# A fused attention and feed-forward kernel: the lag between the two row halves carried through the down tiles and across batches, scales moved to the outputs, plain evictions

## The chip, the cores and the metric

The kernel runs on one core of one Trainium2 chip. The metric is the device time of one execution in microseconds. The kernel before was timed three times: 424.82, 425.56 and 425.59 us, median 425.56. Engines are called as in the profile: PE (TensorE matmuls; PEld its weight loads), DVE (VectorE), ACT (ScalarE), POOL (GpSimd) and SP (SyncE, which issues output and transpose DMAs).

## The reference

Grouped attention (8 batches, 16 query heads on 4 key heads, 384 positions, head size 64) is followed by a feed-forward layer on the 3072 x 1024 result:

```python
scores = (1.0 / np.sqrt(D)) * np.matmul(q, k.transpose(0, 1, 3, 2))
attn = np.exp(scores - np.max(scores, axis=-1, keepdims=True))
attn = attn / (np.sum(attn, axis=-1, keepdims=True) + 1e-09)
x = np.matmul(attn, v).transpose(0, 2, 1, 3).reshape(B * S, H * D)
h = np.maximum(x @ w_in, 0.0)        # w_in 1024 x 2048
out = h * h @ w_out                  # w_out 2048 x 1024
```

## The kernel before, in words

**How the order comes about.** The kernel doesn't issue instructions as it goes. A `Recorder` (line 9) takes each operation with its engine, what it reads and writes, and a cost in us; it keeps a clock for each engine and derives which earlier operations must be waited for. A loop (line 1035) asks at each step which pieces could start next on PE (score bursts `sc`, attention-times-value `av` and `av2`, feed-forward pieces `ffn`) by these clocks and picks one. `emit` (line 86) then writes each engine's list in the recorded order with semaphore waits. So every cost and every clock in the text below is the planner's and shapes the order alone. Each engine runs its list strictly in order.

**Stages.** Batch by batch there is an up stage (x times w_in, relu, square, into `h2T`) and a down stage (`h2T` times `w_out_sb`, into `y_sb` and out by DMA). The attention of later batches is woven in: scores of batch b+1 (`burst_small`, L392, two PSUM banks per burst out of 0 to 3) with their exponentials on ACT (L402), and attention times value (`av_halves`, L459, a pair of banks 0,1 or 2,3, closed by a reciprocal and a product on DVE, L472 and L474). The result goes through a DMA transpose to `xT`.

**Batches 2 to 7, up.** `strassen` (line 695) forms x times w_in by seven products of half size in f16; four sums on DVE (`sums`, L593) prepare its operands. There are 28 units (7 products, two column groups, two units each), each in one of PSUM banks 4 to 7, which it shares in turn with the unit four later. A unit is two halves f, each of four matmuls of 192 columns. The contraction is split by rows: rows 0 to 63 of the PE array (y = 0, the upper half) and rows 64 to 127 (y = 1, the lower half) do separate matmuls that can run beside each other. Both add into the same bank, and the lower half begins a unit only when the upper has ended it: it lags by three pieces. So `part(n)` pairs upper half n with lower half n-3, for n in 0 to 58. In the first three pieces only the upper half has work, in the last three only the lower.

When a unit's lower half ends, `evict` (line 717) moves it from PSUM to one of eight f32 buffers `hr`, multiplied by the scale `unit`, one value per partition. Products 1, 5, 6 are kept (L729), products 3, 7, 2 are multiplied and added to a kept one (L734), product 4 goes alone with its relu (L725). `close_squares` (line 671) then gives relu and square to engines: DVE does both in one instruction (L681), or ACT does the relu (L685) and ACT (L689) or POOL (L692) the square into `h2T`.

**Down.** In batches 2 to 6 (`on_halves`), `down_pair` (line 845) does two output tiles of 128 x 512 at once: in each piece of eight matmuls (L860) the upper row half works on one tile and the lower on the other, without lag, and after four pieces they swap. Three pairs make 24 pieces. In batch 7 there are six full-array tiles (`down_part`, L818). `store` (line 829) copies each bank to `y_sb` (L834) and issues the output DMA on SP's queue.

**POOL** also makes the doubled keys `k_dup` (L300), the values with a ones column `v_aug` (L305, L622), spreads a maximum (L603), and issues the loads of k, q and v; those loads wait for the transposes that read the buffers before.

Of the kernel before, what the change touches and what calls it, by code (L numbers as in the profile page):

```python
# [141 lines left out]
def bass_gqa_attention__then__ffn_squared_relu_kernel(  # L142
# [242 lines left out]
    def burst_small(b, pieces, base):  # L385
# [3 lines left out]
        def sc(pe):  # L389
            for m, (u, _, _) in enumerate(pieces):  # L390
# [8 lines left out]
              cost=total / 2400 + (0.01 if b else 0.2))  # L399
# [9 lines left out]
    def av(b, c, banks):  # L409
# [12 lines left out]
        R.add("tensor", lambda pe: mm(pe, 6 * s2), reads=av_reads(b, c), writes=[("bank", i)], cost=0.285)  # L422
        yield
        R.add("tensor", lambda pe: mm(pe, 6 * s2 + 3), reads=av_reads(b, c), writes=[("bank", i)], cost=0.285)
# [21 lines left out]
    def av_halves(b, c, pairs):  # L446
# [17 lines left out]
        lead = R.add("tensor", lambda pe: mm(pe, 0), reads=av_reads(b, c), writes=keys, cost=0.285)  # L464
        yield lead
        held.difference_update(p)
        R.add("tensor", lambda pe: mm(pe, 1), reads=av_reads(b, c), writes=keys, cost=0.285, after=(lead,))
# [158 lines left out]
    def w_units():  # L626
        R.add("vector", lambda e: e.tensor_scalar(w_unit[:, 0:1], tops[2][:, :], TINY, DOWN, ALU.max, ALU.mult),
              reads=[("tops", 2)], writes=["w_u0"], cost=0.1)
        R.add("vector", lambda e: e.reciprocal(w_unit[:, 1:2], w_unit[:, 0:1]), reads=["w_u0"], writes=["w_u1"], cost=0.1)
        R.add("vector", lambda e: e.tensor_scalar(w_unit[:, 2:3], w_unit[:, 0:1], DOWN, None, ALU.mult),  # L630
              reads=["w_u0"], writes=["w_unit"], cost=0.1)
# [39 lines left out]
    def close_squares(which):  # L671

        for x in [x for x in open_squares if which(x)]:
# [3 lines left out]
            act = max(R.clock["scalar"], R.ops[i]["end"]) + 0.42 * relu  # L677
            dve = max(R.clock["vector"], R.ops[i]["end"]) + 0.6 + 0.6 * bool(ff["now"])
            if dve < min(act + 0.42, max(act, R.clock["gpsimd"]) + 1.0):
                val = val.rearrange("p (f t) -> p f t", f=2)  # L680
                hr_read[r] = (R.add("vector", lambda e, dst=dst, val=val: e.scalar_tensor_tensor(dst, val, 0.0, val, ALU.max, ALU.mult),  # L681
                                    reads=[("hr", r)], writes=keys, cost=0.57),)
                continue
            if relu:
                R.add("scalar", lambda e, val=val: e.activation(val, val, AF.Relu),  # L685
                      reads=[("hr", r)], writes=[("hr", r)], cost=0.42)
            val = val.rearrange("p (f t) -> p f t", f=2)
            if R.clock["scalar"] < R.clock["gpsimd"] + 0.6:
                R.add("scalar", lambda e, dst=dst, val=val: e.activation(dst, val, AF.Square),  # L689
                      reads=[("hr", r)], writes=keys, cost=0.42)  # L690
            else:
                R.add("gpsimd", lambda e, dst=dst, val=val: e.tensor_tensor(dst, val, val, ALU.mult),  # L692
                      reads=[("hr", r)], writes=keys, cost=1.0)

    def strassen(b):
# [18 lines left out]
        kept, ends = {}, {}  # L714
        kap = unit[b % 2][:, 0:1]

        def evict(prod, j, at):
            src = bank(at)[:, 0:S]
            if prod in KEPT or prod == 4:
# [4 lines left out]
                if prod == 4:  # L724
                    R.add("vector", lambda e: e.tensor_scalar(hr[r][:, :], src, kap, 0.0, ALU.mult, ALU.max),  # L725
                          reads=[("bank", at), ("unit", b % 2)], writes=[("hr", r)], cost=0.54, after=hr_read.pop(r, ()))
                else:
                    kept[prod, j] = r
                    R.add("vector", lambda e: e.tensor_scalar(hr[r][:, :], src, kap, None, ALU.mult),  # L729
                          reads=[("bank", at), ("unit", b % 2)], writes=[("hr", r)], cost=0.54, after=hr_read.pop(r, ()))  # L730
                    return
            else:
                r = kept.pop((ADDED[prod], j))
                R.add("vector", lambda e: e.scalar_tensor_tensor(hr[r][:, :], src, kap, hr[r][:, :], ALU.mult, ALU.add),  # L734
                      reads=[("bank", at), ("unit", b % 2), ("hr", r)], writes=[("hr", r)], cost=0.54)
# [5 lines left out]
        def part(n):  # L741

            todo, need, wrote, after = [], [], [], ()
            if n // 2 < len(units):
                todo.append((0, n // 2, n % 2))
            if 0 <= n - 3 < 2 * len(units):
                todo.append((1, (n - 3) // 2, (n - 3) % 2))
            for y, u, f in todo:
                need += OPS[units[u][0]][2]
                wrote.append(("bank", units[u][2]))  # L750

            def piece():
                def mm(pe):
                    for kc in range(k):
                        for y, u, f in todo:
                            prod, j, at = units[u]
                            w, m, _ = OPS[prod]
                            r = slice(64 * y, 64 * y + 64)
                            c = 128 * (2 * j + f)
                            mm = pe.matmul(bank(at)[:, f * h:f * h + h], w[r, kc, c:c + 128], m[r, kc, :],  # L760
                                           start=(prod in (1, 5, 2) and y + f + kc == 0), stop=(y + f == 2 and kc == k - 1), skip_group_check=True)
                    return mm

                lead = [ends[u] for y, u, f in todo if y and f == 0]
# [477 lines left out]
```

## Time and profile before

| | us |
|---|---|
| median of three runs | 425.56 |
| the profiled execution | 424.91 |
| its span, first to last instruction | 423.1 |
| PE busy | 409.8 |
| DVE busy | 286.7 |
| ACT busy | 195.6 |
| POOL busy | 77.2 |
| L860, 960 matmuls, busy | 117.7 |
| L760, 2688 matmuls, busy | 199.1 |
| up stage of batch 4 (232.00 to 259.40): DVE busy | 24.29 of 27.40 |
| down stage of batch 4 (259.40 to 282.85): DVE busy | 7.95 of 23.45 |

Matmuls are pipelined: one of 192 columns shows 243 ns, though the next on the same half starts about 82 ns later. A busy PE in the profile is therefore not yet a PE at its rate, and short waits hide in the busy time; the distance from one start to the next is what counts. The same holds more weakly for DVE: an eviction shows 615 ns, and the next instruction begins 0.52 to 0.66 us after its start. In rows in order of time the columns are start, duration, engine, line, operation, tiles out<-in, shapes, count, and in brackets the idle time before with what ended it.

### The profile page before, as it was taken

Reading aid. Unit: us, or ns where it says so; the run is one execution under the profiler, and the core shown is the slowest. Engines: PE = TensorE matmul, PEld = TensorE weight load, DVE = VectorE, ACT = ScalarE, POOL = GpSimd, SP = SyncE. Lnnn points to the kernel's source line nnn. Section 1 sums busy time; section 2 is a strip of 40 time slices with the busy share of each in tenths; the row PEclk is TensorE's granted clock in tenths of the full one; section 3 lists DMA queues with packets and bytes.
Section 4 is the critical chain, followed back from the end, with each engine's and each line's share of the span. In section 5 each row is a group of like instructions: output and inputs, shape, how many; then the busy total and the mean of one; then the engine's idle time right before and its main releaser. Section 6 shows DMA issues by size and latency. Waiting matters only on the chain.

```text
span 423.1 us, 14792 instructions
## 1 busy us (share of the span) xinstructions
PE 409.8 (97%) x6816; PEld 284.8 (67%) x6816; DVE 286.7 (68%) x540; ACT 195.6 (46%) x261; POOL 77.2 (18%) x100
## 2 busy tenths in 40 slices
PE   8999999989899999999999989999999999999997
PEld 5566654554558875488756887669954699559744
DVE  3699988999796974379652796438943588439712
ACT  6958510275008950494515925259415675004400
POOL 7680000251300321004200233000110012002200
DMA  9999999994981099414991189323622202311012
GB/s 169 180 186 189 206 187 178 254 113 84 169 149 51 3 135 168 101 53 39 165 151 51 53 141 125 89 100 30 114 35 70 101 3 41 78 63 53 3 69 79
DMA packets 96942, 44.73 MB, mean 106 GB/s; under 512 B 77296, under 2 KB 90864, under 8 KB 96880
## 3 DMA queue, kind: packets, MB, share of 16 engines
q0 software_dynamic: 36544, 17.44, 32.5%
q1 hardware_dynamic: 59664, 25.86, 30.3%
q8 instruction: 53, 0.87, 0.9%
q10 hardware_dynamic: 672, 0.49, 0.4%
q14 instruction: 9, 0.07, 0.1%
HBM read 35.65 MB, written 12.58 MB: 114 GB/s over the span
## 4 chain that ended last, share of the span: by engine, by line
PE 80%; DVE 11%; DMA 3%; ACT 2%; POOL 1%; issue 1%; SPq 1%; ACTq 0%; POOLq 0%; DVEq 0%
PE ps L860 24%; PE ps L760 21%; PE ps L818 12%; PE ps L392 7%; PE ps L554 6%; PE ps L459 4%; PE ps L418 3%; DVE hr L734 2%; DVE h2T L681 2%; DMA q_st<-in_q_dram 1%; DMA qT<-q_st 1%; DVE hr L725 1%; PE ps L517 1%; ACT hr L685 1%; ACT h2T L689 1%
## 5 line engine op out<-in xcount | busy, mean ns | idle before, releaser
L402 ACT ACTIVATE expT<-ps 128x1024 bf16<-128x1024 f32 (+1 forms) x145 | 139.5, 1024 | 108.4 <-PE ps L392 106.9
L860 PE MATMUL ps<-w_out_sb,h2T 64*128 64x512 bf16 x960 | 117.7, 376 | 2.1 <-DVE tops L617 1.7
L760 PE MATMUL ps<-xT,w_in_sb 64*128 64x192 f16 x1152 | 82.9, 243 | 1.4 <-DVE hr L734 1.2
L860 PEld LDWEIGHTS ps<-w_out_sb,h2T 64*128 64x128 bf16 x960 | 50.0, 94 | 43.6 <-ACT h2T L689 1.3
L834 DVE COPY y_sb<-ps 128x512 f32<-128x512 f32 (+2 forms) x49 | 31.9, 676 | 62.3 <-PE ps L860 41.3
L760 PEld LDWEIGHTS ps<-xT,w_in_sb 64*128 64x128 f16 x1152 | 70.4, 94 | 4.9 <-DVE hr L734 1.7
L818 PE MATMUL ps<-w_out_sb,h2T 128*128 128x512 bf16 (+2 forms) x304 | 63.6, 368 | 1.1 <-ACT h2T L689 0.6
L685 ACT ACTIVATE hr<-hr 128x384 f32<-128x384 f32 x54 | 27.5, 514 | 56.4 <-DVE hr L734 56.0
L729 DVE TENSOR_SCALAR hr<-ps,unit 128x384 f32<-128x384 f32 x72 | 43.6, 615 | 12.4 <-PE ps L760 10.7
L760 PE MATMUL ps<-s_sum,wx 64*128 64x192 f16 x768 | 50.7, 243 | 0.8 <-DVE hr L725 0.5
L692 POOL TENSOR_TENSOR h2T<-hr 128x384 bf16<-128x384 f32 x21 | 17.3, 826 | 186.6 <-ACT hr L685 186.1
L818 PEld LDWEIGHTS ps<-w_out_sb,h2T 128*128 128x128 bf16 x304 | 28.6, 98 | 33.7 <-ACT h2T L689 1.1
L392 PE MATMUL ps<-qT,kT 64*128 64x256 bf16 (+2 forms) x336 | 50.1, 324 | 0.5 <-ACT expT L402 0.2
L734 DVE SCALAR_TENSOR_TENSOR hr<-ps,unit,hr 128x384 f32<-128x384 f32 x72 | 43.3, 613 | 4.0 <-PE ps L760 2.6
L760 PEld LDWEIGHTS ps<-s_sum,wx 64*128 64x128 f16 x768 | 43.3, 94 | 3.6 <-DVE hr L725 1.8
L554 PE MATMUL ps<-xT,w_in_sb 64*128 64x384 bf16 x448 | 42.5, 323 | 1.3 <-DVE hr L567 1.3
L459 PEld LDWEIGHTS ps<-v_aug,expT 64*128 64x128 bf16 x1440 | 33.3, 94 | 9.3 <-DVE tops L617 0.9
L459 PE MATMUL ps<-v_aug,expT 64*128 64x65 bf16 x1440 | 36.3, 190 | 0.6 <-DVE tops L617 0.4
L760 PE MATMUL ps<-s_sum,w_in_sb 64*128 64x192 f16 x384 | 33.0, 243 | 0.0
L554 PEld LDWEIGHTS ps<-xT,w_in_sb 64*128 64x128 bf16 x448 | 21.5, 94 | 17.0 <-DVE hr L567 2.1
L760 PE MATMUL ps<-xT,wx 64*128 64x192 f16 x384 | 32.5, 243 | 0.0
L472 DVE RECIPROCAL rinv<-ps 128x6 f32<-128x6 f32 x40 | 7.8, 194 | 30.3 <-PE ps L459 30.0
(82 smaller groups left out, 410.4 us busy)
## 6 DMA issues: line engine op xcount, KB each, us to landing
out_dram<-y_sb SPq DMA_DIRECT2D x47, 256.0 KB, 2.2
q_st<-in_q_dram POOLq DMA_DIRECT2D x12, 384.0 KB, 7.7
w_in_sb<-in_moe_w_in_dram POOLq DMA_DIRECT2D x8, 512.0 KB, 14.5
w_out_sb<-in_moe_w_out_dram POOLq DMA_DIRECT2D x4, 1024.0 KB, 29.7
v_st<-in_v_dram POOLq DMA_DIRECT2D x7, 192.0 KB, 8.2
k_st<-in_k_dram POOLq DMA_DIRECT2D x6, 192.0 KB, 5.6
wx<-in_q_dram POOLq DMA_DIRECT2D x2, 384.0 KB, 7.1
q_st<-in_q_dram POOLq DMA_DIRECT2D x3, 192.0 KB, 5.1
```

Source lines behind the costliest of these rows:

```text
L392: mm = pe.matmul(ps[:, base + x, m * wide:(m + 1) * wide], kT[at(b)][64 * x:64 * x + 64, u, :], q_cols(b, u // NJ, x, c0, c0 + wide))
L402: R.add("scalar", lambda e: e.activation(dst, src, AF.Exp, scale=0.125), reads=keys, writes=[("expT", (b * NU + u) % NEX, t) for u, _, _ i ...
L459: m = pe.matmul(ps[:, p[x], n * DP:n * DP + D + 1], w, v_aug[b % 2][r, g * NJ + j, 0:D + 1], start=(n + j + y == 0), stop=(n + j + y == 2 ...
L554: m = pe.matmul(bank(4 + xs[x])[:, 0:S], w_in_sb[r, kc, c * 128:(c + 1) * 128], xT[b % NXT][r, kc, :], start=(phase < 2 and kc == 0), stop ...
L685: R.add("scalar", lambda e, val=val: e.activation(val, val, AF.Relu), reads=[("hr", r)], writes=[("hr", r)], cost=0.42)
L692: R.add("gpsimd", lambda e, dst=dst, val=val: e.tensor_tensor(dst, val, val, ALU.mult), reads=[("hr", r)], writes=keys, cost=1.0)
L729: R.add("vector", lambda e: e.tensor_scalar(hr[r][:, :], src, kap, None, ALU.mult), reads=[("bank", at), ("unit", b % 2)], writes=[("hr", ...
L734: R.add("vector", lambda e: e.scalar_tensor_tensor(hr[r][:, :], src, kap, hr[r][:, :], ALU.mult, ALU.add), reads=[("bank", at), ("unit", b ...
L760: mm = pe.matmul(bank(at)[:, f * h:f * h + h], w[r, kc, c:c + 128], m[r, kc, :], start=(prod in (1, 5, 2) and y + f + kc == 0), stop=(y + ...
L818: m = pe.matmul(bank(i)[:, 0:n], h2T[:, c, i3 * 128:(i3 + 1) * 128], w_out_sb[:, c, c0:c1], start=(c == 0), stop=(c == NFC - 1))
L834: R.add("vector", lambda e: e.tensor_copy(ysl, bank(i)[:, 0:n]), reads=[("bank", i)], writes=[("y", yb)], cost=0.08 + n / 960)
L860: m = pe.matmul(bank(base + x)[:, 0:512], h2T[r, c, i3 * 128:(i3 + 1) * 128], w_out_sb[r, c, jj * 512:(jj + 1) * 512], start=(y + c == 0), ...
```

## The change

- The pieces of the up stage are now built from `Half` objects, the four matmuls of one row half. `zipped(ups, lows)` merges the matmuls of an upper and a lower list by the columns gone by on each side.
- The down tiles of batches 2 to 6, and the first four tiles of batch 7, are halves too (`down_halves`), and the lower half lags the upper by one piece there as well. The last three lower halves of the up stage run beside the first upper half of the down stage. The last lower half of the down stage is carried over and runs beside the first three upper halves of the next batch's up stage. Batch 2 has nothing to carry in, and in batch 7 the last lower half runs alone, followed by two full-array tiles.
- The order in which a down tile takes its sixteen chunks of `h2T` is now 0-3, 8-11, 12-15, 4-7 (before: ascending), and each tile waits only for those column thirds of `h2T` that it reads.
- The scale `unit` leaves the evictions. Kept products are copied as they are, on DVE or, when the planner's clock of ACT is more than 0.3 behind that of DVE, on ACT; sums are plain additions; relu multiplies by a constant. In batches 2 to 7 `store` multiplies by `unit` twice, as h is squared.
- DVE no longer does relu and square in one instruction. It squares only what has its relu (product 4); for the others the plans are ACT and ACT, ACT and POOL, or POOL and POOL (relu by `tensor_scalar`).
- The planner's costs for scores and attention pieces are a little smaller; the free pair of banks is searched in both places, and scores don't take held banks.

```diff
-          cost=total / 2400 + (0.01 if b else 0.2))
+          cost=total / 2400 + (0.004 if b else 0.2))
...
-            if dve < min(act + 0.42, max(act, R.clock["gpsimd"]) + 1.0):
-                hr_read[r] = (R.add("vector", lambda e, dst=dst, val=val: e.scalar_tensor_tensor(dst, val, 0.0, val, ALU.max, ALU.mult),
...
+            plans = [(act + 0.45 * (1 + relu), "ss"), (max(act + 0.52 * relu, pool) + 0.77 + 0.2, "sg")]
             if relu:
+                plans.append((pool + 1.54 + 0.6, "gg"))
+            else:
+                plans.append((dve + 0.49 + 0.4 + 0.6 * bool(ff["now"]), "sv"))
+            one, other = min(plans)[1]
...
-                    R.add("vector", lambda e: e.tensor_scalar(hr[r][:, :], src, kap, 0.0, ALU.mult, ALU.max),
+                    R.add("vector", lambda e: e.tensor_scalar(hr[r][:, :], src, DOWN * DOWN, 0.0, ALU.mult, ALU.max),
...
-                    R.add("vector", lambda e: e.tensor_scalar(hr[r][:, :], src, kap, None, ALU.mult),
+                    if R.clock["scalar"] + 0.3 < R.clock["vector"]:
+                        R.add("scalar", lambda e: e.copy(hr[r][:, :], src),
...
+                        R.add("vector", lambda e: e.tensor_copy(hr[r][:, :], src),
...
-                R.add("vector", lambda e: e.scalar_tensor_tensor(hr[r][:, :], src, kap, hr[r][:, :], ALU.mult, ALU.add),
+                R.add("vector", lambda e: e.tensor_tensor(hr[r][:, :], src, hr[r][:, :], ALU.add),
...
-        return [part(n) for n in range(2 * len(units) + 3)]
+        lag = 3
+        if carried:
+            c = cut(carried)
+            pieces = [zipped([ups[0]], [c[0]]), zipped(ups[1:3], [c[1]])]
+        else:
+            pieces = [zipped([ups[n]], []) for n in range(lag)]
+        for n in range(lag, len(ups)):
+            pieces.append(zipped([ups[n]], [lows[n - lag]]))
+        c = cut(down_up[0])
+        pieces += [zipped([c[0]], [lows[-3]]), zipped([c[1]], lows[-2:])]
+        rest = [zipped([down_up[n + 1]], [down_low[n]]) for n in range(len(down_up) - 1)]
+        if b == B - 1:
+            rest += [zipped([], down_low[-1:])] + downs(b)
+        return pieces, rest, down_low[-1]
+
+    def cut(h):
+        return (Half(h.mms[:1], h.cols, h.need, h.bank, h.first, h.lead),
+                Half(h.mms[1:], h.cols, h.need, h.bank, False, (), h.done))
+
+    CHUNKS = ((0, 1, 2, 3), (8, 9, 10, 11), (12, 13, 14, 15), (4, 5, 6, 7))
...
+            g = unit[b % 2][:, 0:1]
+            R.add("vector", lambda e: e.tensor_scalar(ysl, bank(i)[:, 0:n], g, g, ALU.mult, ALU.mult),
+                  reads=[("bank", i), ("unit", b % 2)], writes=[("y", yb)], cost=0.14 + n / 960)
```

222 lines of the change are left out of this document (126 added, 96 removed).

## The prediction

> **What bounds the kernel now.** I read the page's busy table first, then the chain that ended last, the waits of PE, the stretches by stage, and last the rows in order of time around single waits. Batches 2 to 7 each have an up stage (L760, the seven products) and a down stage (L860 or L818).
>
> ```profile
> PE 409.8 (97%) x6816; PEld 284.8 (67%) x6816; DVE 286.7 (68%) x540; ACT 195.6 (46%) x261; POOL 77.2 (18%) x100
> ```
>
> PE is the bound, so I ask what PE does and where it stops. The chain gives the rate while nothing holds it:
>
> ```profile
> 208.71 0.86 PE ps L860 x8
> 209.58 0.27 PE ps L459 x18
> ...
> 302.80 1.32 PE ps L760 x32
> ```
>
> Eight L860 matmuls are four pairs, one matmul on the upper and one on the lower 64 rows, so 0.216 us for a pair of 512 columns. Thirty-two L760 matmuls are 16 pairs of 192 columns, 0.0825 us each. At such rates I summed the columns of all 6816 matmuls in the program's order, a half that works alone counted like a pair: 396.1 us. The profiled execution took 424.91 us (span 423.1, 1.8 around it), so 28.8 us are no columns. The starts of PE's rows place them: some 14 before the first L760 (loads, batches 0 and 1), 9.4 between there and the end, the rest at the tail and around the span. Batch by batch (2 to 7) the 9.4 are 1.57, 2.57, 2.90, 1.27, 0.12, 0.98.
>
> They are of two kinds. At the turn from up to down PE runs one L860 piece and then waits for DVE's queue; here the chain passes from PE to DVE and back:
>
> ```profile
> 205.41 1.14 DVE hr L725 x2
> 206.55 0.02 issue
> 206.58 0.56 DVE h2T L681
> 207.14 0.21 DVE tops L617
> 207.35 0.05 issue
> 207.40 1.04 PE ps L860 x8
> ```
>
> The five turns cost 1.01, 1.02, 0.49, 0.55, 0.0 and the last one 0.98: 4.05 us. The other 5.35 us lie inside up stages. The largest, 1.07 us, in order of time:
>
> ```profile
> 240.46 0.83 POOL L692 TENSOR_TENSOR h2T<-hr 128x384 bf16<-128x384 f32 x1 [30.67 <-ACT hr L685]
> 241.23 1.46 POOL L300 COPY k_dup<-k_st 128x1536 bf16<-128x1536 bf16 x1
> 241.27 1.83 DVE L681 SCALAR_TENSOR_TENSOR h2T<-hr 128x384 bf16<-128x384 f32 x1
> ...
> 243.69 0.25 PE L760 MATMUL ps<-xT,w_in_sb 64*128 64x192 f16 x1 [0.91 <-DVE hr L734]
> ```
>
> A DVE square that reads hr twice took 1.83 us instead of 0.55, because GpSimd was in a copy of 1.46; the eviction behind it was late, and PE waited for its bank.
>
> **The change, part by part.**
>
> 1. *Lag carried on.* The program's order shows it done. Before, each of the six up stages had 59 pieces of 0.33, of which the first three and last three use one half of the rows; then 24 two-sided down pieces. After, the last three run beside the first upper down piece, and in batches 3 to 7 the first three run beside the last lower one of the batch before. Per batch that hides two one-sided pieces of four matmuls, that is one two-sided piece of 8 matmuls, 0.864 us. Batches 2 to 6 gain it; batch 7 ends with a lower piece alone and gains nothing. 5 x 0.864 = **-4.3**. The same column sum over the changed order is 391.75, which is 4.3 less. What no row shows is a 192-column upper matmul beside a 512-column lower one. Bounds: full overlap as in the equal pairs (0), or none at all, 0.85 us at each of 11 such places (+9.4). I take 0, because both kinds of equal pairs run at their column rate.
>
> 2. *A wait filled.* In batch 1 PE waited 1.48 us at 111.6 for GpSimd's L622, behind query loads that wait for transposes. The new order puts one more down part (0.86) ahead of that place and leaves one fewer behind it, where the sums end at 127.5 and PE arrives at 128.1, about 0.8 earlier now. **-0.9**, between 0 and -0.9.
>
> 3. *Evictions without the pointer.* L729, L734, L725 have the pointer scalar `unit`; L567 is the same shape with an immediate:
>
> ```profile
> L729 DVE TENSOR_SCALAR hr<-ps,unit 128x384 f32<-128x384 f32 x72 | 43.6, 615 | 12.4 <-PE ps L760 10.7
> L734 DVE SCALAR_TENSOR_TENSOR hr<-ps,unit,hr 128x384 f32<-128x384 f32 x72 | 43.3, 613 | 4.0 <-PE ps L760 2.6
> L567 DVE TENSOR_SCALAR hr<-ps 128x384 f32<-128x384 f32 x28 | 14.1, 549 | 2.5 <-PE ps L554 2.5
> ```
>
> 615 against 549 busy; from start to start 0.52 to 0.66 against 0.47. For the add without pointer the nearest row is L474, a product of PSUM and SBUF, 558. A batch has 28 evictions: about 28 x 0.09 = 2.5 us less on DVE, plus three squares fewer (1.4) and one copy on ACT. DVE is off PE's path except at stalls, so this pays only there. It should clear the turns: DVE there runs about 1 us behind, and the first down chunks now read tiles finished early. I leave 0.2 per turn: 4.05 to 1.2, **-2.9** (bounds 0 and -4.05).
>
> 4. *Relu and square.* DVE squares (L681) fall from 23 to 16; GpSimd now does relu and square in a row for 18 of the 96. No row shows its relu; the nearest are its cast of 128x384 (511 ns) and its two-input square (826), far ends 0.45 and its 128x1536 copy (1.67); I take 0.8, nearest the same size. ACT gets 10 squares more and 8 copies, about 9 us in six batches, beside 195.6 busy of 423; in the order exps are not behind them for long, so 0.
>
> 5. *What is late next.* A bank is reused three pieces (1.0 us) after its last matmul, and an eviction needs 0.2 + 0.55, so DVE can slip only 0.2 us. In batches 3 to 5 GpSimd gets three relu-square chains and, right behind them, the k_dup copy. By columns from batch 3's start: the product-3 and product-7 tiles that go to GpSimd are added by 8.4 and 9.3, the third at 11.5; 1.65 per chain puts their end at 13.5, then 1.46 of k_dup until 15.0. DVE's two squares come at 13.3 and 14.2, in the middle of that. The first slips 0.25 and puts k_dup off to 15.4, the second waits for k_dup, the eviction behind it ends at 16.4, and PE needs its bank at 15.1: about 1.4 us of stall, the picture of 241.27 again. Batch 2 has four chains and by the same sum 0.6. 3 x 1.4 + 0.6 + 0.5 for the rest = 5.3, as much as the 5.35 that go: **0** (bounds -4.8 if they miss each other, +4 if each square is caught).
>
> The Trainium skill ("SBUF — State Buffer", Terms, shared port pair) says that VectorE and GpSimd share a port pair that one instruction holds to its end while the other blocks wholly; 241.27 agrees (1.83 = 1.4 of waiting + 0.4). "GPSIMD Engine Reference", Specifications, limits this to DVE instructions in a two-port mode or with two SBUF inputs; the rows agree too, L729 at 143.97 and 195.39, inside a GpSimd copy of 1.79, kept 0.62. By its introduction (VectorE is roughly twice as fast in elementwise work) a GpSimd relu would be an estimated 0.9 to 1.1 us and the clash 0.3 to 0.9 later; the sum would stay.
>
> 6. *Outputs scaled.* 36 evictions y_sb get two pointers: 687 ns plus 0.06 to 0.2, beside L860 work where DVE is busy 7.95 of 23.45 us. On the path only at the end, with the first full-array tile of batch 7 waiting for a bank: **+0.3** (0 to 0.5).
>
> Sum: 424.9 - 4.3 - 0.9 - 2.9 + 0 + 0.3 = **417.1 us**. The profiled execution is 0.65 below the median of the runs (425.56) and inside their spread, so I leave the number as it is.
>
> **The rivals.**
>
> - *DVE and GpSimd miss each other.* GpSimd's chains end earlier, or k_dup waits. For it: of the 23 old squares one was caught badly (1.83), four by 0.1 to 0.2, the others not at all. Then 4.8 us more go: 412.3.
> - *Only the lag pays.* Turns and stalls stay, since a shorter instruction doesn't shorten a queue in wrong order, or unequal pairs overlap partly. For it: DVE's slack of 0.2 us. 424.9 - 4.3 = 420.6, less 0.9 if the filled wait counts; half of the 9.4 on top gives 424.
> - *Slower: DVE's squares caught each time.* Place: the DVE squares in up stages, behind GpSimd's relu, square, k_dup and v_aug. Price: 0.8 to 1.46 us for each hit, one to one on PE. Without any such stall the sum is 412.3; it takes 12.6 us, 2.1 per batch over six, to undo it. Three squares per batch at 1.46 would be 4.4. Beyond 2.1 the kernel is slower, about 427. Against it: the third square lies at the stage's end, where GpSimd is idle by the order, and batches 6 and 7 have no k_dup.
> - *It doesn't do what it says.* Excluded for the lag, by the order.
>
> **How the numbers follow.** Forecast (415 to 419.5): 0.48. Missed clash (411 to 415): 0.25. Only the lag (419.5 to 424): 0.2. Slower: 0.06. The range takes the first two and half of the third: 411.5 to 422, 8 in 10. Runs of this kernel differ by under 0.2%, which is the bound for "same". Faster 0.92, same 0.02, slower 0.06.
>
> **What would show it.** L860's successor should have 23 two-sided pieces between up stages. Between the last product and the second two-sided down piece no wait of PE over 0.3. DVE evictions near 0.55 busy. In batches 3 to 5 a DVE square of over 1 us beside GpSimd's k_dup copy, and a PE wait of about 1.4 behind it; if these squares keep 0.55, part 5 is wrong and the time is near 412. Unequal pairs that take over 0.97 us for 768 upper plus 1536 columns would prove part 1 wrong.

## The result, and the profile after

The changed kernel takes 418.79 us in the median of four runs (418.06 to 420.07), beside 425.57 for the kernel before in the same job: a ratio of 0.985, 95% interval 0.982 to 0.988. Run once more later, beside other kernels on another chip, it came to 419.51, a ratio of 0.987 (0.985 to 0.989). The forecast was 417.1, with a range of 411.5 to 422. The size is about right. The sum behind it is not: one term did not come at all, one is credited to the wrong part of the change, and the largest saving is mostly eaten elsewhere.

The profiled execution took 418.33 us with a span of 416.4. Its busy table, to be held against that of before:

```profile
PE 405.7 (97%) x6873; PEld 292.6 (70%) x6880; DVE 275.2 (66%) x525; ACT 203.4 (49%) x279; POOL 100.3 (24%) x115
```

DVE has 11.5 us less to do, POOL 23.1 more. The groups show where both come from (busy us, mean ns of one, then the idle time ahead):

```profile
L690 POOL TENSOR_SCALAR hr<-hr 128x384 f32<-128x384 f32 x18 | 28.2, 1565 | 183.0 <-DVE hr L782 183.0
...
L782 DVE TENSOR_TENSOR hr<-ps,hr 128x384 f32<-128x384 f32 x72 | 39.6, 556 | 14.5 <-PE ps L798 11.7
...
L777 DVE COPY hr<-ps 128x384 f32<-128x384 f32 x64 | 34.9, 556 | 13.7 <-PE ps L798 9.7
```

An eviction without the pointer takes 556 ns, where L729 and L734 took 615 and 613. GpSimd's relu takes 1565 ns, twice the 0.8 us that the prediction gave it. The chain of waits at batch 3's turn from up to down, where before it went over DVE (start, length, what):

```profile
202.18 0.08 PE ps L847
202.27 0.16 PE ps L798 x2
202.43 0.08 PE ps L847
202.51 0.08 PE ps L798
202.60 0.00 PE ps L613
202.60 0.08 PE ps L798
202.68 1.68 PE ps L847 x16
```

L798 is now the product piece, L847 the down piece, and L613 spreads a maximum for the next batch. The two kinds of piece alternate, and DVE no longer stands in the chain. The twelve trailing lower product matmuls start at 201.53 and end at 202.52: 0.99 us, twelve times the 0.0825 of an equal pair. The four upper down matmuls that run beside them cost nothing.

A word on comparing profiles. The first 22 us, loads and transposes, differ by up to 2.6 us from one profile to another, by 0.4 between the two of the changed kernel. So I compare the stretch from the first product matmul to the end of the span. It fell from 294.5 to 288.6 us. Its columns, at the rates of the prediction, take 281.7 before and 277.4 after, so what is not columns fell only from 12.9 to 11.2. In the second profile of the changed kernel these are 288.9 and 11.5.

The stretch, too, differs between executions of one kernel. Now and then PE stops inside a run of matmuls that has no semaphore to wait for, and the profile names no releaser ("issue"). Such gaps come to 1.1 us in this profile, to 1.45 in the second one of the same kernel, and to between 0 and 2.0 in those of the other runs; what causes them is open. So a difference of 1 to 2 us between two stretches says little unless gaps with a named releaser account for it.

Adding up PE's gaps over 0.1 us in that stretch (from one start to the next, less the columns of the first) places most of the rest. Turns: 0.62 in batch 2 and 0.37 in batch 7, 0.98 in all (before 4.05). Inside up stages: 3.2 (before 5.35). Ahead of the first full-array tile of batch 7: 0.44. And 3.2 in a place that had next to none, the down stages. These 3.2 are of three kinds.

The first, 1.0 us in four gaps, is PE waiting for banks that DVE has yet to empty, where attention pieces stand next to each other. One in order of time:

```profile
313.02 1.15 PE L459 MATMUL ps<-v_aug,expT 64*128 64x65 bf16 x47
...
313.66 0.56 DVE L474 TENSOR_TENSOR o_sb<-ps,rinv 128x384 f16<-128x384 f32 x1
...
314.28 0.60 PE L847 MATMUL ps<-w_out_sb,h2T 64*128 64x512 bf16 x4
```

Eighteen L459 matmuls are one half of an attention piece, 0.27 us; DVE's two instructions for a whole piece (L472, L474) need 0.7. The down piece L847 that follows needs the banks that L474 reads. It starts 0.06 us after L474 has ended, 0.27 later than the columns ahead of it would allow. The second kind, 1.1 us in five gaps of 0.22, is the second half of an attention piece that waits for the end of the first, since both add into the same banks; where the halves stand apart, a down piece fills that time. In the changed order three or four attention halves stand together in each down stage of batches 2 to 5, and both kinds come from that: 2.1 us. The third kind, 0.71 and 0.40, are gaps without a releaser. The larger one, in this profile:

```profile
263.35 0.62 PE L459 MATMUL ps<-v_aug,expT 64*128 64x65 bf16 x27
...
264.13 0.56 DVE L474 TENSOR_TENSOR o_sb<-ps,rinv 128x384 f16<-128x384 f32 x1
264.53 0.81 PE L459 MATMUL ps<-v_aug,expT 64*128 64x65 bf16 x27 [0.55 <-issue]
```

In the second profile it ends with this row:

```profile
264.64 0.82 PE L459 MATMUL ps<-v_aug,expT 64*128 64x65 bf16 x27 [1.07 <-issue]
```

It looks like the first kind and is not. It stands in the middle of a half (27 matmuls are one half and nine more), and PE goes on while L474 is still running. From start to start it is 0.71 in the first profile and 1.23 in the second, and the one of 0.40 is not in the second.

### The profile page after: what moved, and what is told of

Same layout as the page of the kernel before. It is cut to its first block, busy times and chain, and to the rows that moved or that the text cites. A ratio compares the mean times of both kernels' runs of the same rounds, so it can differ in the third digit from the quotient of the medians.

```text
span 416.4 us, 14931 instructions
## 1 busy us (share of the span) xinstructions
PE 405.7 (97%) x6873; PEld 292.6 (70%) x6880; DVE 275.2 (66%) x525; ACT 203.4 (49%) x279; POOL 100.3 (24%) x115
## 4 chain that ended last, share of the span: by engine, by line
PE 82%; DVE 9%; ACT 2%; DMA 2%; issue 2%; POOL 1%; SPq 1%; POOLq 0%; DVEq 0%
PE ps L847 27%; PE ps L798 25%; PE ps L903 7%; PE ps L392 7%; PE ps L554 5%; PE ps L459 5%; PE ps L418 3%; ACT expT L402 2%; DMA qT<-q_st 1%; PE ps L517 1%; DVE hr L567 1%; DVE hr L777 1%; DVE wx L648 1%; DVE wx L653 1%; DMA wx<-in_k_dram 1%
## 5 line engine op out<-in xcount | busy, mean ns | idle before, releaser
L847 PE MATMUL ps<-w_out_sb,h2T 64*128 64x512 bf16 x1088 | 140.3, 376 | 0.8 <-issue 0.2
L847 PEld LDWEIGHTS ps<-w_out_sb,h2T 64*128 64x128 bf16 x1088 | 64.9, 94 | 37.9 <-issue 0.7
L798 PE MATMUL ps<-xT,w_in_sb 64*128 64x192 f16 x1152 | 82.5, 243 | 0.2 <-DVE xT L593 0.2
L798 PEld LDWEIGHTS ps<-xT,w_in_sb 64*128 64x128 f16 x1152 | 71.8, 94 | 5.0 <-PE ps L798 1.2
L690 POOL TENSOR_SCALAR hr<-hr 128x384 f32<-128x384 f32 x18 | 28.2, 1565 | 183.0 <-DVE hr L782 183.0
L924 DVE TENSOR_SCALAR y_sb<-ps,unit 128x512 f32<-128x512 f32 (+2 forms) x37 | 29.3, 794 | 36.2 <-PE ps L847 30.3
L798 PE MATMUL ps<-s_sum,wx 64*128 64x192 f16 x768 | 51.1, 243 | 0.8
L903 PE MATMUL ps<-w_out_sb,h2T 128*128 128x512 bf16 (+2 forms) x233 | 48.6, 364 | 0.7 <-DVE y_sb L924 0.3
L782 DVE TENSOR_TENSOR hr<-ps,hr 128x384 f32<-128x384 f32 x72 | 39.6, 556 | 14.5 <-PE ps L798 11.7
L798 PEld LDWEIGHTS ps<-s_sum,wx 64*128 64x128 f16 x768 | 44.0, 94 | 4.2 <-DVE hr L777 2.8
L777 DVE COPY hr<-ps 128x384 f32<-128x384 f32 x64 | 34.9, 556 | 13.7 <-PE ps L798 9.7
L459 PEld LDWEIGHTS ps<-v_aug,expT 64*128 64x128 bf16 x1440 | 37.2, 94 | 8.8 <-DVE tops L617 0.9
L554 PE MATMUL ps<-xT,w_in_sb 64*128 64x384 bf16 x448 | 42.1, 323 | 0.7 <-DVE hr L567 0.6
L903 PEld LDWEIGHTS ps<-w_out_sb,h2T 128*128 128x128 bf16 x240 | 22.4, 98 | 25.1 <-DVE y_sb L924 0.5
L459 PE MATMUL ps<-v_aug,expT 64*128 64x65 bf16 x1440 | 37.4, 190 | 1.3 <-issue 0.6
L554 PEld LDWEIGHTS ps<-xT,w_in_sb 64*128 64x128 bf16 x448 | 21.4, 94 | 16.7 <-DVE hr L567 1.8
L798 PE MATMUL ps<-s_sum,w_in_sb 64*128 64x192 f16 x384 | 32.9, 243 | 0.1
L693 ACT ACTIVATE h2T<-hr 128x384 bf16<-128x384 f32 x62 | 31.6, 521 | 1.7
L798 PE MATMUL ps<-xT,wx 64*128 64x192 f16 x384 | 31.8, 243 | 0.1
```

Source lines behind the costliest of these rows:

```text
L459: m = pe.matmul(ps[:, p[x], n * DP:n * DP + D + 1], w, v_aug[b % 2][r, g * NJ + j, 0:D + 1], start=(n + j + y == 0), stop=(n + j + y == 2 ...
L554: m = pe.matmul(bank(4 + xs[x])[:, 0:S], w_in_sb[r, kc, c * 128:(c + 1) * 128], xT[b % NXT][r, kc, :], start=(phase < 2 and kc == 0), stop ...
L690: R.add("gpsimd", lambda e, val=val: e.tensor_scalar(val, val, DOWN * DOWN, 0.0, ALU.mult, ALU.max), reads=[("hr", r)], writes=[("hr", r)] ...
L693: R.add("scalar", lambda e, dst=dst, two=two: e.activation(dst, two, AF.Square), reads=[("hr", r)], writes=keys, cost=0.45)
L777: R.add("vector", lambda e: e.tensor_copy(hr[r][:, :], src), reads=[("bank", at)], writes=[("hr", r)], cost=0.48, after=hr_read.pop(r, ()))
L782: R.add("vector", lambda e: e.tensor_tensor(hr[r][:, :], src, hr[r][:, :], ALU.add), reads=[("bank", at), ("hr", r)], writes=[("hr", r)], ...
```

## The experiments

All kernels but the probe are edits of the changed one. "Rest" is the stretch described above less its columns.

| run | lag | evictions | median us | ratio to before (95%) | stretch | rest |
|---|---|---|---|---|---|---|
| before | no | pointer | 425.57 | 1 | 294.5 | 12.9 |
| changed | yes | plain | 418.79 | 0.985 (0.982 to 0.988) | 288.6 | 11.2 |
| after_again | yes | plain | 419.51 | 0.987 (0.985 to 0.989) | 288.9 | 11.5 |
| no_lag | no | plain | 419.75 | 0.988 (0.986 to 0.989) | 289.6 | 7.9 |
| pointer | yes | pointer | 420.29 | 0.988 (0.986 to 0.990) | 289.9 | 12.6 |
| ptr_no_lag | no | pointer | 423.24 | 0.996 (0.994 to 0.998) | 293.2 | 11.5 |
| chunks | yes | plain | 428.31 | 1.008 (1.004 to 1.012) | 299.3 | 22.0 |
| half_relu | yes | plain | 423.02 | 0.996 (0.994 to 0.997) | 292.9 | 15.6 |
| anypair | yes | plain | 418.18 | 0.983 (0.981 to 0.986) | 286.6 | 9.2 |
| spread | yes | plain | 414.39 | 0.974 (0.972 to 0.977) | 283.3 | 6.0 |
| spread_no_lag | no | plain | 420.10 | 0.989 (0.987 to 0.992) | 289.8 | 8.1 |
| spread_ptr | yes | pointer | 414.39 | 0.976 (0.974 to 0.978) | 284.8 | 7.5 |
| best | yes | plain | 414.63 | 0.977 (0.974 to 0.979) | 285.5 | 8.2 |

### after_again: the changed kernel once more

> The changed kernel once more, beside the others on one chip. Theory: 418.5 us, give or take 0.7, and the same waits as in its first profile (8.4 us between the first product piece and the end); what differs lies in the first 22 us, where the profiles so far differ by up to 2.4 us. Rival (the waits themselves vary from run to run): other places or sizes of PE's waits behind 130 us.

419.51 us, 0.3 above the theory's span of 417.8 to 419.2. PE's gaps behind 130 us that have a named releaser are the same ones, at the same places and of the same size. Those without one differ: 0.71 became 1.23, 0.40 is gone, and 0.22 is new. All over 0.1 make 8.1 us (7.7 in the first profile). So a gap with a releaser is the kernel's, one without may belong to a single execution, and a difference of less than 1 us between medians of two runs is not to be relied on.

### no_lag: the lag taken out

```diff
-        if carried:
-            c = cut(carried)
-            pieces = [zipped([ups[0]], [c[0]]), zipped(ups[1:3], [c[1]])]
-        else:
-            pieces = [zipped([ups[n]], []) for n in range(lag)]
+        pieces = [zipped([ups[n]], []) for n in range(lag)]
...
-        pieces += [zipped([c[0]], [lows[-3]]), zipped([c[1]], lows[-2:])]
-        rest = [zipped([down_up[n + 1]], [down_low[n]]) for n in range(len(down_up) - 1)]
+        pieces += [zipped([], [lows[n]]) for n in range(len(lows) - lag, len(lows))]
+        rest = [zipped([down_up[n]], [down_low[n]]) for n in range(len(down_up))]
```

> The changed kernel, but each batch's three leading upper pieces and three trailing lower pieces run alone again, and the down pieces have no lag; evictions, relu on GpSimd and scaled outputs stay as changed. Its column sum is 396.07 us against 391.75. Theory (the lag is worth its columns, and unequal pairs overlap fully): 418.8 + 4.3 = 423.1 us, with no other difference between the stages. Rival (the lag packs the attention pieces into the down stage and so caused the new waits of 3.2 us there, which eat part of its gain): these waits shrink with the lag gone, 420 to 421.5 us.

419.75 us. The theory falls, and the time is even below the rival's: with 4.3 us more columns the kernel is 0.2 to 1.0 us slower than the changed one by the medians, 0.7 to 1.0 by the stretch. The rest is 3.3 us smaller than with the lag. Gaps over 0.1 us account for 2.3 of that: among the attention pieces of the down stages 0.5 instead of 2.1, without a releaser none instead of 1.1, at the turns 0.4 instead of 1.0; against these, ahead of the first full-array tile of batch 7, 1.29 instead of 0.44. So the rival is right about the place, but of its 3.2 us only 1.6 are shown to come from the lag. In its order, batches 4 and 5 have six attention halves in the up stage and ten in the down stage; with the lag it is four and twelve, and the last three stand together.

### pointer: the scale back in the evictions

```diff
-    R.add("vector", lambda e: e.tensor_copy(hr[r][:, :], src),
+    R.add("vector", lambda e: e.tensor_scalar(hr[r][:, :], src, kap, None, ALU.mult),
...
-    R.add("vector", lambda e: e.tensor_tensor(hr[r][:, :], src, hr[r][:, :], ALU.add),
+    R.add("vector", lambda e: e.scalar_tensor_tensor(hr[r][:, :], src, kap, hr[r][:, :], ALU.mult, ALU.add),
```

The other two evictions likewise; relu multiplies by 1, outputs are copied.

> The changed kernel, with every instruction in the changed order on every engine, but the evictions carry the pointer scale again (and the outputs are plain copies). Theory (plain evictions cleared the turns, about 2.9 us, as the prediction's step 3 has it): turns wait 3 to 4 us again, 421 to 422 us. Rival (the turns went because the lag and the new order of the down chunks give the last tiles more time, whatever an eviction takes): 418.5 to 419.3 us, DVE evictions at 0.61 and turns still near 1 us in all.

420.29 us, between the theory's time and the rival's. The order of instructions is that of the changed kernel on every engine, so this prices the length of the evictions alone: they are worth about 1.2 us here (stretch 1.0 to 1.3). But not at the turns: PE's gaps there are 0.68 in batch 2 and 0.43 in batch 7, none in 3 to 6, as in the changed kernel. What grew are gaps inside up stages, in batches 3 to 5 from 0.30, 0.24 and 0.18 to 0.42, 0.30 and 0.30. So step 3's saving at the turns is not owed to the evictions.

### chunks: the old order of the chunks

```diff
-    CHUNKS = ((0, 1, 2, 3), (8, 9, 10, 11), (12, 13, 14, 15), (4, 5, 6, 7))
+    CHUNKS = ((0, 1, 2, 3), (4, 5, 6, 7), (8, 9, 10, 11), (12, 13, 14, 15))
```

> The changed kernel, but the down halves take their chunks of h2T in the order 0 to 15 (two chunk groups swapped back), as the kernel before did; everything else stays. Theory (what cleared the turns is the new order of the chunks, which reads the tiles finished last at the end, and not the shorter evictions: in the run pointer the turns stayed as short as in the changed kernel): turns wait 1.5 to 2.4 us in batches 2 to 5 and about 2 in batch 7, 424 to 428 us. Rival (the turns went with the shorter evictions, as the prediction's step 3 has it, and pointer kept them short by chance): turns stay under 0.7 us each, 418.5 to 420 us.

428.31 us in the median, slower than the kernel before. The two of its six executions that kept the full clock took 425.43 and 425.63 us, about level with it (424.78 in the same job); the four others, at a granted clock of 0.992 to 0.996, took 428.3 to 431.75. Turns cost 2.34, 1.45, 1.45, 1.45, 0.56 and 2.09 us. The chain of waits at batch 3's turn shows DVE's whole queue between two attention pieces of PE:

```profile
202.79 0.29 PE ps L459 x17
...
203.11 0.21 DVE rinv L472
...
203.34 0.56 DVE o_sb L474
203.90 0.47 DVE hr L782
204.36 0.95 DVE hr L769 x2
205.31 0.46 DVE h2T L697
205.77 0.21 DVE tops L617
...
206.03 0.45 PE ps L459 x18
```

What releases PE is L617, which reads the banks that the next attention half needs, and DVE comes to it last. Chunks 4 to 7 come from products 2 and 4, the last to be done. In the old order the second down piece reads them. In the new order they are read last, so PE finds other work while DVE clears this queue. That is what emptied the turns: 8.4 of the 10.7 us by which the stretch is longer lie there. The rest is a DVE square held up by GpSimd's square ("caught") in each of batches 3 to 6 (0.90 us each), a lower clock in batch 7 (1.6, below) and a gap of 2.0 without a releaser in batch 4; the gaps among the attention pieces are nearly gone. That the lag makes the order of the chunks matter more, since before three lower half pieces ran alone ahead of the turn and gave DVE time, is argued from 9.3 beside the 4.05 of before; it was not run by itself.

### ptr_no_lag: neither lag nor plain evictions

The edits of no_lag and of pointer together, so what is left of the change is the chunk order, the new plans for relu and square, the copies on ACT and the smaller planner costs.

> No lag as in no_lag, and the evictions with the pointer scale and plain outputs as in pointer, in no_lag's order on every engine. Theory (DVE's slack in the up stages decides what an eviction's 0.06 us more is worth, with or without the lag): 421 to 422.5 us, some 1.5 to 2.5 above no_lag's 419.75. Rival (plain evictions pay only where the lag has taken DVE's slack): 419.5 to 420.3 us.

423.24 us, 3.5 above no_lag. But the pair differs by more than the evictions. The edits change what the planner sees, too (a plain output has a lower price there than a scaled one), and against the expectation the order did not stay no_lag's: GpSimd has 21 relus instead of 19, DVE 16 squares instead of 14, and a square is caught in each of batches 3 to 6, where no_lag has one caught in all. The one of batch 4:

```profile
243.07 0.83 POOL L697 TENSOR_TENSOR h2T<-hr 128x384 bf16<-128x384 f32 x1
243.25 1.06 DVE L697 TENSOR_TENSOR h2T<-hr 128x384 bf16<-128x384 f32 x1
...
245.75 0.83 PE L799 MATMUL ps<-s_sum,wx 64*128 64x192 f16 x16 [1.53 <-DVE hr L778]
```

In batches 3 to 6 PE waits 1.1, 1.9, 1.0 and 1.0 us inside up stages (no_lag 0.9, 0.8, 0.8 and 0.5), and a gap of 1.33 in this profile has no releaser. So the 3.5 us are the price of the longer evictions and of these caught squares together, and neither the theory nor the rival is decided. The same holds for the lag under pointer evictions, 3.0 us (423.24 to 420.29). Only pointer and spread_ptr, which keep their partner's order, price the evictions alone. What this run does show is the turns: without the lag and with the pointer in the evictions they cost 0.14 us in all, beside 4.05 before.

### half_relu: a shorter relu on GpSimd

```diff
-    e.tensor_scalar(val, val, DOWN * DOWN, 0.0, ALU.mult, ALU.max)
+    e.tensor_scalar(val[:, 0:192], val[:, 0:192], DOWN * DOWN, 0.0, ALU.mult, ALU.max)
```

> The changed kernel in the changed order, but GpSimd's relu works on 192 of the 384 columns (the other half of those 18 tiles is neither scaled nor clipped). Theory (a longer relu than predicted moved the k_dup copy behind DVE's squares, and only so was the clash of step 5 missed): the relu takes about 0.8 us, the copy starts some 2 us earlier than 194.6, meets a DVE square in batches 3 to 5, that square takes over 1 us, and the time rises by 1 to 4 us, to 420 to 423. Rival (DVE's squares are not held up by GpSimd in this kernel, or hardly): no square over 0.7 us, 418.3 to 418.9 us.

This kernel leaves out part of the computation: the other half of each of those 18 tiles stays as it was. 423.02 us, as the theory has it. The relu now takes 0.85 us, close to what the prediction assumed. In order of time (GpSimd and DVE, and PE's rows that waited):

```profile
193.33 0.82 POOL L697 TENSOR_TENSOR h2T<-hr 128x384 bf16<-128x384 f32 x1
...
193.59 0.98 DVE L697 TENSOR_TENSOR h2T<-hr 128x384 bf16<-128x384 f32 x1
...
194.10 1.79 POOL L300 COPY k_dup<-k_st 128x1536 bf16<-128x1536 bf16 x1
...
195.15 1.16 DVE L697 TENSOR_TENSOR h2T<-hr 128x384 bf16<-128x384 f32 x1
...
197.02 0.83 PE L798 MATMUL ps<-s_sum,wx 64*128 64x192 f16 x16 [0.68 <-DVE hr L777]
```

Both squares of DVE are caught, one by GpSimd's square and one by the k_dup copy. PE loses 0.74, 0.86 and 0.20 us in each of batches 3 to 5 (0.30, 0.24 and 0.18 in the changed kernel); the stretch is 4.0 to 4.3 longer, of which at most 0.6 is a difference in gaps without a releaser. Compare the changed kernel, with the full relu:

```profile
191.19 0.83 POOL L697 TENSOR_TENSOR h2T<-hr 128x384 bf16<-128x384 f32 x1
...
191.89 0.55 DVE L697 TENSOR_TENSOR h2T<-hr 128x384 bf16<-128x384 f32 x1
191.98 1.81 POOL L690 TENSOR_SCALAR hr<-hr 128x384 f32<-128x384 f32 x1
...
193.02 0.55 DVE L697 TENSOR_TENSOR h2T<-hr 128x384 bf16<-128x384 f32 x1
...
194.64 1.46 POOL L300 COPY k_dup<-k_st 128x1536 bf16<-128x1536 bf16 x1
```

Here both squares fall beside the relu and keep 0.55. The copy comes when DVE's squares are done.

### probe: GpSimd and DVE beside each other

A kernel of DVE's and GpSimd's instructions of this case on constants, alone and in pairs; it computes nothing of the reference.

> No part of the computation: DVE's and GpSimd's instructions of this case alone and beside each other, on constants, zeros go to the output. Theory (what blocks a DVE square is a GpSimd copy or two-input product, not its relu): beside GpSimd's relu a square takes 0.55 us in the mean and the relu grows from 1.49; beside GpSimd's square or copy some squares take 0.9 to 1.9 us. An eviction from PSUM, plain (0.55) or an addition, keeps its time beside all of them. Rival (any GpSimd instruction holds the port to its end): squares beside the relu take up to 1.5 us more too. Second rival (an eviction that adds also reads hr and so needs the port): the addition is held up as the square is.

The groups of five stretches: relu alone (L193); DVE squares (L190) beside the relu, beside GpSimd's square (L199), beside its copy (L202); DVE's addition from PSUM (L214) beside the copy.

```profile
L193 POOL TENSOR_SCALAR p_to<-hr 128x384 f32<-128x384 f32 x4 | 5.9, 1496 | 43.2 <-DVE to L223 43.2
...
L193 POOL TENSOR_SCALAR p_to<-hr 128x384 f32<-128x384 f32 x5 | 8.7, 1763 | 0.1
L190 DVE TENSOR_TENSOR h2T<-hr 128x384 bf16<-128x384 f32 x14 | 8.2, 655 | 18.4 <-POOL k_dup L202 18.4
...
L190 DVE TENSOR_TENSOR h2T<-hr 128x384 bf16<-128x384 f32 x7 | 7.1, 1088 | 0.0
L199 POOL TENSOR_TENSOR p_h2T<-hr 128x384 bf16<-128x384 f32 x6 | 6.7, 1146 | 1.7 <-DVE to L205 1.7
...
L190 DVE TENSOR_TENSOR h2T<-hr 128x384 bf16<-128x384 f32 x7 | 11.0, 1633 | 0.0
L202 POOL COPY k_dup<-k_st 128x1536 bf16<-128x1536 bf16 x6 | 10.5, 1800 | 1.9 <-DVE to L205 1.9
...
L202 POOL COPY k_dup<-k_st 128x1536 bf16<-128x1536 bf16 x5 | 7.1, 1471 | 3.7 <-DVE h2T L190 3.7
L214 DVE TENSOR_TENSOR to<-ps,hr 128x384 f32<-128x384 f32 x14 | 6.6, 546 | 0.0
```

A square that takes 0.55 alone takes 1.18 beside each GpSimd square and 1.81 beside each copy, and the two engines strictly alternate. Beside the relu most squares keep 0.55 and about one for each relu takes 0.85; the theory had the mean at 0.55, it is 655 ns. An addition with one operand from PSUM keeps 546 beside the copy, and so do both beside all other kinds: the second rival falls.

The Trainium skill ("SBUF — State Buffer", the part on the two separate sides) calls the pair an exclusive lock for the whole instruction, which a DVE instruction with two SBUF inputs needs only against a GpSimd instruction that reads SBUF. Copy, square and the untouched addition agree; the relu, which reads SBUF too, holds a square up by only 0.3 us of its 1.5, so for it the measurement decides against the page.

### anypair: either free pair of banks for attention

```diff
-            places = [p for p in PAIRS[...] + PAIRS[...] if not held & set(p)][:1] if on_halves(b - 1) else spare
+            places = [p for p in PAIRS[...] + PAIRS[...] if not held & set(p)] if on_halves(b - 1) else spare
```

> The changed kernel, but an attention half may take either free bank pair and not only the next one in turn; the order then has 5 instead of 4 of a batch's attention pieces in the up stage, 10 instead of 12 in the down stage and no three of them back to back there. Theory (the new waits of 3.2 us in down stages come from attention pieces that stand back to back and outrun DVE's two instructions each): those waits fall under 1 us, 415.5 to 417 us. Rival (DVE is as late with these pieces in the up stage, where it has 17.5 us of work already): the waits move there, 418.5 to 419.5 us.

418.18 us: by the median no verdict between 415.5 to 417 and 418.5 to 419.5. The profile, of the fastest of its five executions (416.37), tells more. The gaps among attention pieces in down stages fall from 2.1 to one of 0.63, as the theory has it, and the stretch by 2.0 to 2.3; this profile has no gaps without a releaser, though, where the changed kernel has 1.1 and 1.45. In return the shifted order puts a DVE square into GpSimd's square, in each of batches 3 to 6:

```profile
190.83 0.83 POOL L697 TENSOR_TENSOR h2T<-hr 128x384 bf16<-128x384 f32 x1
...
190.95 1.12 DVE L697 TENSOR_TENSOR h2T<-hr 128x384 bf16<-128x384 f32 x1
...
192.78 0.42 PE L798 MATMUL ps<-s_sum,wx 64*128 64x192 f16 x6 [0.74 <-DVE hr L777]
```

Each costs PE 0.90 us. So both remaining causes show in one kernel, and the next edit goes at both.

### spread, spread_no_lag, spread_ptr: the arrangement mended

```diff
-                plans.append((dve + 0.49 + 0.4 + 0.6 * bool(ff["now"]), "sv"))
+                plans.append((max(dve, R.clock["gpsimd"] if R.clock["gpsimd"] > dve - 0.3 else 0.0) + 0.49 + 0.4 + 0.6 * bool(ff["now"]), "sv"))
...
-  since >= AMONG * (1 + (ff["b"] >= SB))
+  since >= 3
```

(and 3 in the second place that has this condition).

> The changed kernel with two changes in its planner: in up stages an attention piece after every third product piece instead of every fourth, and a square goes to DVE only at a price that counts GpSimd's queue. Theory (the lag's gain was eaten by waits that the arrangement of attention pieces and squares makes, not by the lag itself): PE's waits between the first product piece and the end fall from 8.4 to some 4, the time to 414 to 415 us. Rival (PE waits for DVE wherever the pieces stand, since the lag left it 4.3 us less): waits of 7 or more, 417.5 us or above.

> As the run spread, but without the lag: the leading and trailing product pieces run alone. Theory (with the arrangement mended the lag is worth its columns): 4.3 to 5 us above spread, 418.5 to 420 us. Rival (the lag is worth about 1 us however the pieces stand, as no_lag's 419.75 beside the changed kernel's 418.8 has it): 0.5 to 1.5 us above spread.

> As spread, in its order on every engine, but with the evictions' pointer scale and plain outputs. Theory (an eviction's length costs PE only where a DVE square or two attention pieces stand in the same queue; spread has hardly such places): within 0.7 us of spread's 414.4. Rival (plain evictions are worth 1.3 us or more in any arrangement, as pointer beside the changed kernel): 415.5 to 417 us.

spread takes 414.39 us, a ratio to before of 0.974 (0.972 to 0.977), 4.4 to 5.1 us faster than the changed kernel. DVE squares fall from 16 to 7 and none is caught; of the attention halves in batches 3 to 6 five stand in the up stage, one at the turn and ten in the down stage. Gaps over 0.1 us in the stretch add up to 2.6 (7.7 in the changed kernel, 1.1 of them without a releaser); the profile is of its fastest execution, 412.18. Without the lag the same arrangement takes 420.10: now the lag is worth 5.7 us, its 4.3 of columns and more. That is above the theory's 4.3 to 5 by 0.7, and far from the rival's 0.5 to 1.5. The wait ahead of the first full-array tile of batch 7, 1.29 instead of 0.44, makes 0.85 of what exceeds the columns. With the pointer back it is 414.39 again (0.9 us slower by the two ratios, whose intervals overlap, and 1.5 by the stretches of the two profiles, of which 0.85 are gaps without a releaser), so here plain evictions are worth 0 to 0.9 us. Which of spread's two edits brings how much was not taken apart; anypair, where one of the two waits went and the other came, suggests that each has its share.

### best: the wait in batch 1

```diff
-        R.add("gpsimd", lambda e: e.tensor_scalar(ones_b,
+        R.add("vector" if b == 2 else "gpsimd", lambda e: e.tensor_scalar(ones_b,
```

with spread's edits and anypair's.

> As spread, and an attention half may take either free pair of banks, and the values' unit for batch 2 (L622) is written by DVE instead of GpSimd. Theory on step 2 (PE's wait of 1.3 to 1.5 us in batch 1 hangs on GpSimd's L622, behind query loads and DVE's scaling of the weights): that wait goes, and with waits of about 4 behind the first product piece the time is 413 to 414 us. Rival (something else is as late there, the scaling of the weights on DVE or the values themselves): the wait stays over 1 us, 414.5 to 415.5 us.

414.63 us, no better than spread: 413.29 to 416.42 beside 412.18 to 414.79. On step 2 it gives a clear answer. In the changed kernel the waits of PE list

```profile
PE ps L418 <- POOL v_aug L622: 1.3, 1, 1.3
```

and in this one PE has no wait between 105 and 125 us. So L622 on GpSimd was the cause. What that gains is lost again in batch 2: a gap of 1.24 us at 152.9, ended by GpSimd's L603, which stands there behind a relu, a square and a copy, and one of 0.91 at 176.9, ended by DVE's sums (L593), which had waited for a transpose.

## Why the prediction was right, step by step

1. *Lag carried on, -4.3.* On PE it holds: the columns are 4.3 less, and unequal pairs run at the rate of the busier half (0.99 us for twelve lower matmuls; my mark for a disproof, 0.97, was a little below what twelve equal pairs take, and nothing of the feared 0.85 a place is there). On the clock it does not hold: beside no_lag the lag gained 0.2 to 1.0 us. With the lag, the planner put more attention pieces into the down stage, where halves that stand together wait for L474 and for each other (2.1 us, in no_lag 0.5). This wait is in none of my steps. With the pieces spread the lag is worth 5.7.
2. *A wait filled, -0.9.* Wrong. The wait is still there, 1.28 by the waits and 1.45 from start to start (before 1.48). From the first L554 matmul to the first product piece it took 99.6 us before, 99.4 and 99.7 in the two profiles after.
3. *Turns cleared by plain evictions, -2.9.* The size is right (4.05 to 0.98), the cause is not. The order of the chunks does it, which I named in half a sentence and did not price: without it turns cost 9.3 us, and with it they are clear even where the evictions keep the pointer (1.1 us in pointer, 0.14 in ptr_no_lag). Plain evictions save their time elsewhere, inside up stages: about 1.2 us in the changed order, 0 to 0.9 in spread's. Nor did DVE gain what I counted: an eviction became 0.06 us shorter (556 ns beside 615), not 0.09, and three squares fewer hold for batches 2 and 3 alone, seven in all.
4. *Relu on GpSimd, 0.8 us.* It measured 1.565; 1.67, the bound on that side, was nearer. I chose by the size of the tile. What in this instruction takes the time, its two operations or something else, no run shows.
5. *What is late next, 0.* This step failed. I predicted that a square in batches 3 to 5 takes over 1 us beside the k_dup copy; all kept 0.55. The mechanism is real, as half_relu shows with a relu of 0.85: squares of 0.98 and 1.16, and 4 us. It was the size in step 4 that moved the copy behind the squares. So 5.35 us in up stages became 3.2, not 5.3, and 3.2 came back in the down stages, 2.1 with a releaser and 1.1 without. The two mistakes nearly cancel, and that is luck.
6. *Outputs scaled, +0.3.* L924 takes 0.80 for 512 columns, 0.12 more than L834's copy; a gap of 0.44 stands at the place named, ahead of the first full-array tile of batch 7. With plain outputs (pointer) the gap there is still 0.32, so most of it is not the scale's.

The rival *DVE and GpSimd miss each other* described what happened in the up stages, and its 412.3 failed by the waits in the down stages that it didn't have either. *Only the lag pays* is refuted: in this arrangement it is the part that paid least. *Slower* did not come from squares, but a form of it was close: chunks shows that the change without the reordered chunks is 0.8% slower than the kernel before in the median, and level with it at full clock.

## What to carry to other kernels

When the busiest engine is given less work, the engine behind it keeps its own, and the gain is paid out only as far as that one's bursts fit into the shorter stage: space them anew before judging the cut (here the same cut was worth about 1 us, and 5.7 after respacing). Take apart a change with several parts by undoing each, the incidental one too: the chunks' new order carried some 8 us at the turns alone. Where a planner sets the order, undoing one part can rearrange the rest, as in ptr_no_lag: two runs price a part only if their orders agree. Call a gap a wait for another engine only if the profile names what ended it; one that changes between two profiles of one kernel is not to be put down to its order. Last, when a forecast has two engines collide at a certain moment, the duration of everything queued ahead decides whether they do, so such a term should be carried as both cases, not as its middle.

## What the runs showed of the hardware

GpSimd's `tensor_scalar` with two operations on 128x384 of f32 takes 1.49 us alone, its two-input square 0.83 and DVE's square 0.55. Its half, 192 columns, takes 0.85, so 0.64 us for 192 columns more, or 3.3 ns a column. The Trainium skill ("GPSIMD Engine Reference", Engine selection) has one-input work on GpSimd roughly at line rate; these rows, of an instruction with two operations, disagree.

DVE's start-to-start times in the probe: 0.47 us for a plain copy, an immediate scale or an addition of 384 columns, 0.52 to 0.53 with a pointer; for 512 columns 0.60 as a copy and 0.72 with two pointers.

In chunks PE waited 2.1 us at the turn of batch 7, and for the next 4 us the granted clock was lower (in the table by stretches the clock is the third from last column):

```profile
400.60:402.80 2.20, 0.27 (x7) 0.05 (x3) 1.31 (x3) 1.61 (x4) 2.05 (x2) 1.00 0.00 0
402.80:406.80 4.00, 4.00 (x22) 1.54 (x24) 0.00 (x0) 0.00 (x0) 0.00 (x0) 0.57 0.01 4
406.80:411.00 4.20, 4.20 (x42) 1.88 (x40) 0.00 (x0) 0.00 (x0) 0.00 (x0) 1.00 0.00 0
```

Eight pairs of 512 columns started 0.42 us apart instead of 0.213, which is 1.6 us lost on top of the wait. A wait of 2.34 us in batch 2 of the same execution, and a gap of 2.0 in batch 4, had no such consequence (clock 1.00). The Trainium skill ("TensorE: Matmul & The Clock Gate", What's actually happening) has the clock halved after an idle window of about 3.4 us whose phase runs free; 0.42 fits its halved rate, and the wait here was shorter than that window. Why one wait in three trips it stays open.
